# A static order for four interleaved layers on one core: overlapping durations in its planner, 28 more exponential pairs on VectorE, new due times

## The chip, the cores and the metric

The kernel runs on one core of a Trainium2 chip. The metric is the device time of one execution in microseconds. The kernel before took 2329.83 us (median of 3 runs, 2328.9 to 2332.01).

## The reference

```python
x = A_x                                     # 1 x 2048 x 1024, bf16
x = x + A(layernorm(x)); x = x + B(layernorm(x))
x = x + A(layernorm(x)); x = x + B(layernorm(x))

# A: linear attention, 32 heads of 32
q, k, v = split(x @ wqkv)
phi(t) = concat(softmax(t @ w_phi), softmax(-t @ w_phi))
kv = sum_s phi(k) v ; z = sum_s phi(k)
A = (phi(q) kv) / (phi(q) z + 1e-6) @ wo

# B: softmax attention, 32 heads of 32
p = softmax(q k^T / sqrt(32)) ; B = (p v) @ wo
```

Each layer pair has weights of its own kind (A's and B's), and both pairs use the same ones.

## The kernel before

The residual stream lies in SBUF, turned (features on partitions), as `xT`. The program is not written in the order in which it runs. The code makes a list of small steps (`op`: engine, assumed duration, what it needs, the buffers it takes, a due time called `prio`). Then `Sched.run` lays them out once, while the program is built: it follows an assumed clock, gives each engine, when it is free, the ready step with the earliest due time for which SBUF and PSUM have room, and writes the steps out in that order. On the chip each engine works through its own fixed list, held only by semaphores. So an assumed duration never runs on the chip. It only changes the order.

The work around the change is layer B's attention, done twice (once in each pair of layers):

- The 32 heads are 8 groups `g` of four, the 2048 queries 4 chunks `qc` of 512. One (qc, g) is a **turn**; there are 32 in each attention. A turn has two halves (`pp`), each of 32 **units**. A unit is a score block of 128 keys by 512 queries of one head.
- Three units make a score group: three matmuls of 32 rows each (L1124) into three PSUM banks. There are two such sets of three banks, used in turn. ScalarE takes the exponential of all three in one instruction of 1536 columns (L1140). There are 1366 of these, 683 in each attention, so a turn has 21 1/3 of them.
- Some units are handed to VectorE. The table `COUNT` says how many **pairs** of units each turn hands over, `HOST` after how many units of the half they are placed. A handed unit rides in a score group with two others, and ScalarE's instruction is then 1024 columns wide. VectorE reads its bank (the **take**, L1055). After two takes it finishes the pair by a polynomial on 1024 columns: L1063, L1067 twice, L1070, each needing the one before. The tiles between (`xg`, `xx`) exist once, the takes' result (`xu`) five times.
- The exponentials are multiplied into the values, and into ones for the denominator (L1172: four column groups of PE at once, in bank 6). After each half VectorE copies the sums out (L1188). The denominators go through small DMAs on SyncE's queue and a reciprocal (L1225), and L1232 divides.
- PE also does projections for coming turns through bank 7, again in four column groups (L499): K, Q and V (VectorE evacuates them in L940, L948, L964), the output projection, and in the first attention the next layer A's keys. Their due times are `KP`, `KGAP` (K), `VQ` (V), `QA`, `LATE` (Q), `OUT1`, `OP0`, `OGAP` (output), `AK` (next layer's keys), and, for the first projections of an attention, `LATER`; `OUT` is layer A's own output. The weights for them come by DMAs that POOL and SyncE issue (L601, L604).
- Where PE has nothing ready in an attention, the planner puts in a padding step (matmuls whose result is not used: `idle` and `idle_acc`, L1407 to L1416).

Before, the planner let an engine's next step begin when the one before it ended, with `dve_us(n) = n/960 + 0.15` and `act_us(n) = n/1200 + 0.064` us.

Of the kernel before, what the change touches and what calls it, by code (L numbers as in the profile page):

```python
# [11 lines left out]
ACT = mybir.ActivationFunctionType  # L12
# [34 lines left out]
LAT = {"PE": 0.2, "ACT": 0.08, "DVE": 0.1, "POOL": 0.2, "SP": 2.0, "AQ": 2.0, "GQ": 2.5}  # L47
SWITCH = 0.1
AGAIN = 0.2
RING = 0.5  # L50
TIE = 7
LOOK = 8
# [2 lines left out]
class Sched:  # L55
# [99 lines left out]
    def run(self):  # L155
# [6 lines left out]
        busy = {e: 0.0 for e in engines}  # L162
        mode = {e: None for e in engines}
        events = []
        n = 0
# [21 lines left out]
        t, left, order = 0.0, len(self.ops), []  # L187
        while left:
            moved = False
            for e in engines:  # L190
                if busy[e] > t + 1e-9 or not ready[e]:
                    continue
                skipped = []
                pick = None
                full = e == "PE" and self.live.get("E", 0) >= FULL
                while ready[e] and len(skipped) < 400:
                    item = heapq.heappop(ready[e])
                    if full and not item[3].first:
                        full = False
                        held = [i for i in ready[e] if i[3].drain] if not item[3].drain else []  # L200
                        best = min(held, key=lambda i: i[:3], default=None)
                        if best is not None and self._alloc(best[3].bufs):
                            ready[e].remove(best)
                            heapq.heapify(ready[e])
                            heapq.heappush(ready[e], item)
                            pick = best[3]
                            break
                    if item[3].along and (mode[e] != item[3].mode or item[3].rows[0] in rows) and item[3].prio > now - DUE:
                        skipped.append(item)
                        continue  # L210
                    if item[3].prio <= todo[front] + WINDOW and self._alloc(item[3].bufs):
                        pick = item[3]
                        break
                    skipped.append(item)
                for s in skipped:
                    heapq.heappush(ready[e], s)
                if pick is None and e == "PE" and self.idle is not None and self.live.get("S", 0):

                    recent = [r for r in recent if r[1] > t - SPELL]
                    worked = sum(r[1] - max(r[0], t - SPELL) for r in recent)  # L220
                    if worked >= KEEP * SPELL:
                        pass
                    elif self.bank_used[7]:

                        if accum:
                            pick = Op("PE", MM, LAT["PE"], self.idle_acc, (), 0.0, "c", 0)
                            left += 1
                    elif not self.live.get("fil", 0):
                        pick = Op("PE", MM, LAT["PE"], self.idle, (Buf("ps", 0, "idle", [(7,)]),), 0.0, "c", 0)
                        pick.bufs[0].left = 1  # L230
                        self.queue["idle"] = [list(pick.bufs), 0]
                        assert self._alloc(pick.bufs)
                        left += 1
                if pick is None:
                    continue
                if pick.first:
                    now = pick.prio
                if e == "PE":
                    recent.append((t, t + pick.dur))
                    if pick.accum is not None:  # L240
                        accum = pick.accum
                d = pick.dur
                if pick.along and (mode[e] != pick.mode or pick.rows[0] in rows):
                    d += AGAIN
                if e == "PE":
                    rows = pick.rows
                if pick.mode is not None:
                    if mode[e] is not None and mode[e] != pick.mode:
                        d += SWITCH
                    mode[e] = pick.mode  # L250
                pick.start = t
                if pick.fn not in (self.idle, self.idle_acc):
                    started[pick.prio] = started.get(pick.prio, 0) + 1
                while front < len(todo) - 1 and started.get(todo[front], 0):
                    started[todo[front]] -= 1
                    front += 1
                busy[e] = t + d
                order.append(pick)
                left -= 1
                moved = True  # L260
                n += 1
                heapq.heappush(events, (t + d, n, pick, True))
                n += 1
                lat = pick.lat
                if e in ("SP", "AQ", "GQ"):
                    ring = max(ring, t + d) + (lat - LAT[e]) * RING
                    lat = LAT[e] + ring - t - d + pick.slack
                heapq.heappush(events, (t + d + lat, n, pick, False))
            if moved:
                continue  # L270
            if not events:
                stuck = [(o.prio, o.eng, [(b.cls, b.at) for b in o.bufs]) for e in engines for _, _, _, o in ready[e]][:8]
                raise AssertionError(f"nothing can start at {t:.1f}: {left} left, {stuck}, live {self.live}")
            t = events[0][0]
            while events and events[0][0] <= t + 1e-9:
                _, _, o, own = heapq.heappop(events)
                if not own:
                    for b in o.bufs:
                        b.left -= 1
                        if b.left == 0:  # L280
                            self._release(b)
                for x in o.out:

                    if own != (x.eng == o.eng and x.eng not in ("SP", "AQ", "GQ")):
                        continue
                    x.ndep -= 1
                    if x.ndep == 0:
                        heapq.heappush(ready[x.eng], (not (x.first or x.along), x.prio - x.ahead, x.seq, x))
# [7 lines left out]
LONG = {"kT", "v", "slab", "slabk", "xn", "xn1", "kvacc", "kvm", "zm", "wnat"}  # L296
MODEST = {"slabk", "xn1", "e1", "vp1", "pkf", "lnw1", "w2o"}
NUMS = 2
LATER = ((20, 20, 0, 0), (20, 20, 0, 0))
VQ = (((1, 4.5), (36, 4), (70, 6)), ((1, 8), (70, 9), (140, 6)))  # L300
FULL = 5
OUT = (26, 22)
EARLY = (0.0, 0.0)
DUE = 0.0
BOOST = 20.0
EVAC = 20.0
QA = (90.0, 6.0)
KVG = 0.14
QUOTA = {"pk": 3, "pv": 2, "kv": 1, "ln": 2, "mm": 4, "cmp": 2, "bc": 4, "num": NUMS, "wt": 4, "fil": 2,
         "e": 6, "vp": 6, "e1": 4, "vp1": 4, "E": 6, "q2": 3, "kt": 3, "w2": 6, "w2o": 3, "oT": 27, "T": 4, "den": 2,  # L310
# [8 lines left out]
POW2_Z = 4  # L319
POW2_S = 0.07634790955  # L320
POW2_C = (-9.003200807141349, 20.025741504269316)
HOST = ((), (14,), (7, 18), (3, 12, 21), (2, 9, 16, 23))
SIDE = (2, 4)
HALF = 4
KGAP = (4, 6)
LATE = 10.0
KP = (0, 16, 56, 92, 122, 146, 170, 192)
BO = 225
OP0 = (243, 263, 287)
OGAP = (2.4, 2.4, 2.4)  # L330
COUNT = ((0,) * 3 + (2,) * 9 + (3,) * 5 + (2,) * 4 + (1,) * 4 + (2,) * 6 + (0,),
         (0,) + (2,) + (4, 3) * 12 + (2,) * 5 + (0,))
PAIRS = ((), ((0, 2),), ((0, 2), (1, 2)), ((0, 1), (0, 5), (1, 3)), ((0, 1), (0, 5), (1, 1), (1, 5)))
AK = ((0, 190), (1, 220), (2, 265))
OUT1 = ((163, 1.5), (176, 1.5), (251, 1.5))


def act_us(n):
# [3 lines left out]
def dve_us(n):  # L342
    return n / 960 + 0.15
# [6 lines left out]
def kernel(  # L350
# [148 lines left out]
            nc.tensor.matmul(out_[ks, :], lhsT=lhsT[:, ks], rhs=rhs, start=start, stop=stop,  # L499
                             tile_position=(0, 32 * k), skip_group_check=True)  # L500

    MM4 = 0.225

    def kind(pb):

# [182 lines left out]
    def a_keys(c, base, wk_s, wv_s, kv, banks, alone=False, step=0.1):  # L688
        xb, xv, fin = xnA[c]
        kv_b, kv_v, kv_last = kv  # L690
        for fc in range(2):
# [3 lines left out]
            for t in range(TB):  # L695
# [7 lines left out]
                if alone:  # L703
# [8 lines left out]
                red = op("DVE", dve_us(1024), lambda ev=ev, sv=sv: nc.vector.reduce_sum(  # L712
                    out=sv(), in_=ev().rearrange("p s (h d) -> p (s h) d", d=DH), axis=AX.X),
                    ex, [eb, sb_], pr)
                rc = op("DVE", 0.39, lambda sv=sv: nc.vector.reciprocal(out=sv(), in_=sv()), [red], [sb_], pr)
                pr_v = pr + (1.01 * step if alone else 0.01)
                vp, vpv = ps("fil" if alone else "pv", banks)
                v1 = mmg2(vp, vpv, lambda po, ts=ts: xv()[:, po, ts], lambda po, vw=vw: vw()[:, po, :],
# [77 lines left out]
    def split_hl(w_b, w_v, dep, prio):  # L796

        h_b, h_v = sb("hl", C512)
        s_b, s_v = sb("hl", C512)
        a = op("DVE", 0.42, lambda: nc.vector.tensor_copy(out=h_v(), in_=w_v()), [dep], [w_b, h_b], prio)  # L800
        b = op("DVE", dve_us(512), lambda: nc.vector.scalar_tensor_tensor(
            out=s_v(), in0=h_v(), scalar=hl[:, 0:1], in1=w_v(), op0=ALU.mult, op1=ALU.add),
            [a], [w_b, h_b, s_b], prio)
        return s_b, s_v, b
# [273 lines left out]
    def attention(base, kT, vT, q_of, gate, extra):  # L1078
# [69 lines left out]
        if True:  # L1148
            for qc, g in turns:
                T = []  # L1150
                end = (qc, g) == turns[-1]
                for pp in range(2):
# [5 lines left out]
                    for n, (d, u) in enumerate(order):  # L1158
                        prio = base + 10 * pos[(qc, g)] + 5 * pp + 0.5 * (n // 2)
                        if True:  # L1160
# [17 lines left out]
                            ebs = [e_of[us[0]][0]]  # L1178
                            if e_of[us[1]][0] is not ebs[0]:
                                ebs.append(e_of[us[1]][0])  # L1180
                            last = op("PE", 0.225, fn, flat([last, ex_of[us[0]], ex_of[us[1]], v_done[(kc % 4, g % 4 // 2)]]),
                                      [a_b, v_b, *ebs], prio - 1, mode="c")
                            last.accum = n != 15
                            last.drain = True
# [37 lines left out]
                    [T[k][2]], [c_b, T[k][0]], kb=2) for k in range(2) for i in range(2)]  # L1222
                for o in m:
                    o.slack = 1.5
                rc = op("DVE", 0.27, lambda c_v=c_v: nc.vector.reciprocal(out=c_v(), in_=c_v()), m, [c_b], prio)  # L1225
                aw = dma(prio, lambda c_v=c_v, at_d=at_d: nc.sync.dma_start(
                    out=at_d.rearrange("h (s c) -> (h s) c", c=16), in_=c_v()), [rc], [c_b], kb=8)
                bk = dma(prio, lambda r_v=r_v, at_d=at_d: nc.sync.dma_start(
# [221 lines left out]
```

## Time and profile before

| | before |
|---|---|
| median of 3 runs | 2329.83 us |
| the profiled execution, whole | 2329.07 us |
| its span, first to last instruction | 2327.3 us |
| granted TensorE clock | 0.997 |
| PE busy | 2223.1 us, 96% |
| ScalarE (ACT) busy | 2032.8 us, 87% |
| VectorE (DVE) busy | 1738.1 us, 75% |
| exponentials on ACT (L1140) | 1366, of them 308 with 1024 columns |
| takes on DVE (L1055) | 306, that is 153 pairs |

The busy share of an engine is the time in which at least one of its instructions is under way. ACT and DVE begin an instruction before the one in front has ended, so the durations of a group may add up to more than its busy time. PE's matmuls are pipelined, and their ends are modelled.

### The profile page before, as it was taken

What the parts mean: (1) busy time and instruction counts of PE and PEld (TensorE: products, weight loads), DVE (VectorE), ACT (ScalarE), POOL (GpSimd) and SP (SyncE); (2) the same over time, 40 slices, a digit from 0 to 9 for tenths busy, and PEclk for the clock granted to TensorE, in tenths of its full rate; (3) what the DMA queues carried; (4) which work ended last, traced back from release to release, by engine and by line L of the source; (5) the groups of instructions that cost most, each with busy time, mean ns of one, the idle gap of its engine ahead of it and who ended that gap; (6) DMA issues with size and microseconds to landing.
All of it is one profiled execution on the core that took longest, in us unless ns stands there. A gap on an engine that the chain in (4) does not pass through costs nothing. (4 is left out here: it accounts for less than half of the span.)

```text
span 2327.3 us, 68705 instructions
## 1 busy us (share of the span) xinstructions
PE 2223.1 (96%) x30156; PEld 872.5 (37%) x30220; DVE 1738.1 (75%) x2213; ACT 2032.8 (87%) x1921; POOL 182.8 (8%) x280
## 2 busy tenths in 40 slices
PE   7999999999999999999999999999999999999998
PEld 4443344444333333333333434433333333333333
DVE  7986762566678768577875776599999999888664
ACT  4436569999999999999997555799999999999997
POOL 0110000000011010111123200000000000100000
PEclk9999999999999999999999999999999999999999
DMA  9220101111132121122224100111110110201111
GB/s 204 55 62 1 33 15 39 41 37 39 45 83 76 48 76 56 62 98 70 83 90 140 43 16 13 24 34 32 30 34 21 40 31 25 66 29 32 46 37 36
DMA packets 124262, 118.80 MB, mean 51 GB/s; under 512 B 60729, under 2 KB 102713, under 8 KB 123577
## 3 DMA queue, kind: packets, MB, share of 16 engines
q1 hardware_dynamic: 105848, 60.38, 9.9%
q0 software_dynamic: 16032, 51.92, 7.9%
q8 instruction: 236, 3.87, 0.7%
q10 hardware_dynamic: 2080, 2.10, 0.3%
q14 instruction: 66, 0.53, 0.1%
HBM read 78.71 MB, written 14.14 MB: 40 GB/s over the span
## 5 line engine op out<-in xcount | busy, mean ns | idle before, releaser
L1140 ACT ACTIVATE arena<-psum 128x1536 bf16<-128x1536 f32 (+1 forms) x1366 | 1712.5, 1488 | 16.0 <-PE psum L1124 10.5
L1172 PE MATMUL psum<-arena 128*32 128x512 bf16 x4096 | 624.3, 384 | 4.8 <-DVE arena L1188 3.1
L1172 PE MATMUL psum<-arena,ones_bf 128*32 128x512 bf16 x4096 | 624.7, 384 | 1.8 <-issue 1.8
L499 PE MATMUL psum<-arena 128*32 128x512 bf16 (+1 forms) x10304 | 609.0, 349 | 4.0 <-DVE arena L1010 1.7
L1124 PE MATMUL psum<-arena 32*128 32x512 bf16 x4096 | 536.9, 382 | 57.5 <-ACT arena L1140 48.8
L495 PE MATMUL psum<-arena 128*128 128x512 bf16 (+1 forms) x1976 | 436.3, 368 | 15.2 <-issue 4.6
L1124 PEld LDWEIGHTS <-arena 32*128 32x128 bf16 x4096 | 179.0, 91 | 576.8 <-issue 567.9
L1067 DVE SCALAR_TENSOR_TENSOR arena<-arena 128x1024 f32<-128x1024 int32 (+1 forms) x306 | 373.6, 1221 | 11.5 <-PE psum L1124 1.5
L499 PEld LDWEIGHTS <-arena 128*32 128x32 bf16 x10304 | 234.9, 96 | 230.2 <-issue 115.9
L1055 DVE TENSOR_SCALAR arena<-psum 128x512 int32<-128x512 f32 x306 | 208.7, 686 | 104.7 <-PE psum L1124 96.1
L495 PEld LDWEIGHTS <-arena 128*128 128x128 bf16 x2032 | 189.5, 98 | 239.6 <-issue 50.3
L1172 PEld LDWEIGHTS <-arena 128*32 128x32 bf16 x4096 | 162.7, 95 | 229.9 <-issue 180.9
L1070 DVE SCALAR_TENSOR_TENSOR arena<-arena 128x1024 int32<-128x1024 f32 x153 | 186.3, 1218 | 2.8
L940 DVE CAST arena<-psum 128x512 bf16<-128x512 f32 x128 | 87.8, 686 | 121.0 <-PE psum L499 100.1
L1172 PEld LDWEIGHTS <-ones_bf 128*32 128x32 bf16 x4096 | 159.3, 95 | 26.5 <-issue 12.7
L601 POOL DMA_DIRECT2D arena<-in_B_wqkv_dram x46 | 40.8, 889 | 1289.3 <-ACT arena L1140 202.7
L1188 DVE COPY arena<-psum 128x512 f32<-128x512 f32 x126 | 86.5, 687 | 59.8 <-PE psum L1172 47.2
L708 ACT ACTIVATE arena<-psum 128x512 bf16<-128x512 f32 x80 | 43.1, 599 | 82.7 <-PE psum L495 61.0
L1063 DVE TENSOR_SCALAR arena<-arena 128x1024 int32<-128x1024 int32 x153 | 105.4, 689 | 5.0 <-PE psum L1172 1.5
L834 ACT ACTIVATE arena<-psum 128x512 bf16<-128x512 f32 x128 | 69.7, 596 | 33.0 <-PE psum L495 30.4
L499 PE MATMUL psum<-xT,onesD 128*32 128x512 bf16 x1044 | 97.1, 382 | 0.8 <-DVE arena L721 0.7
L587 DVE TENSOR_TENSOR arena<-xT,arena 128x1024 f32<-128x1024 bf16 x64 | 77.9, 1218 | 25.0 <-ACT arena L576 24.5
(108 smaller groups left out, 1400.6 us busy)
## 6 DMA issues: line engine op xcount, KB each, us to landing
arena<-rd SPq DMA_DIRECT2D x62, 256.0 KB
arena<-in_B_wqkv_dram POOLq DMA_DIRECT2D x58, 256.0 KB, 4.0
arena<-in_B_wo_dram POOLq DMA_DIRECT2D x40, 256.0 KB, 4.2
arena<-arena SPq DMA_DIRECT2D x256, 32.0 KB
arena<-wd_k POOLq DMA_DIRECT2D x32, 256.0 KB, 4.6
arena<-in_A_wqkv_dram POOLq DMA_DIRECT2D x32, 256.0 KB, 3.9
arena<-arena SPq DMA_DIRECT2D x96, 64.0 KB
out_dram<-arena SPq DMA_DIRECT2D x32, 128.0 KB
```

Source lines behind the costliest of these rows:

```text
L495: nc.tensor.matmul(out_, lhsT=lhsT, rhs=rhs, start=start, stop=stop, skip_group_check=True)
L499: nc.tensor.matmul(out_[ks, :], lhsT=lhsT[:, ks], rhs=rhs, start=start, stop=stop, tile_position=(0, 32 * k), skip_group_check=True)
L587: s1 = op("DVE", dve_us(1024), lambda pr=pr, w_v=w_v: nc.vector.tensor_tensor(out=w_v(), in0=xT[:, pr, csl(c)], in1=m_v().unsqueeze(1).to_ ...
L940: return op("DVE", dve_us(512), lambda: nc.vector.tensor_copy(out=dst(), in_=src()), [dep], bufs, prio)
L1055: o = op("DVE", dve_us(512), lambda: nc.vector.tensor_scalar(out=y_v()[:, k, :].bitcast(I32), in0=s_v()[:, x * C512:(x + 1) * C512], scala ...
L1063: last = op("DVE", 1024 / 1920 + 0.15, lambda: nc.vector.tensor_scalar(out=z_v().bitcast(I32), in0=y_v().bitcast(I32), scalar1=0x7FFFFF, s ...
L1067: last = op("DVE", dve_us(1024), lambda i=i, c=c: nc.vector.scalar_tensor_tensor(out=x_v(), in0=(x_v() if i else z_v().bitcast(I32)), scal ...
L1070: return op("DVE", dve_us(1024), lambda: nc.vector.scalar_tensor_tensor(out=y_v().bitcast(I32), in0=x_v(), scalar=POW2_S / BITS ** 2, in1= ...
L1124: nc.tensor.matmul(out=s_v()[:, x * C512:(x + 1) * C512], lhsT=kT[g][1]()[r, pp, d * P:(d + 1) * P], rhs=q_of[(qc, g)][1]()[r, (pp + j // ...
L1140: ex = op("ACT", act_us(w * C512), lambda s_v=s_v, e_v=e_v, w=w: nc.scalar.activation(out=e_v(), in_=s_v()[:, 0:w * C512], func=ACT.Exp, s ...
L1172: nc.tensor.matmul(out=a_v()[col:col + 32, :], lhsT=v_v()[:, kc % 4, o:o + DH] if what == 0 else ones_bf[:], rhs=ev()[:, x * C512:(x + 1) ...
L1188: cp = op("DVE", dve_us(512), lambda t_v=t_v, a_v=a_v: nc.vector.tensor_copy(out=t_v(), in_=a_v()), [last], [a_b, t_b], prio - 4)
```

## The change

The planner now frees DVE 0.085 us and ACT 0.012 us before a step's assumed end, and holds a dependent step of the same engine back by 0.03 and 0.13 us after it. Some assumed durations are set anew. `COUNT` hands over 28 more pairs: 15 in the first attention (57 to 72), 13 in the second (96 to 109). All due times listed above are set anew. No instruction is changed in itself; the work is the same but for the 28 pairs, and 381 padding steps of PE instead of 387. The lines of the kernel's body move down by 7 (L1140 becomes L1147).

```diff
+OVER = {"DVE": 0.085, "ACT": 0.012}
+NEXT = {"DVE": 0.03, "ACT": 0.13}
...
-                busy[e] = t + d
+                busy[e] = t + d - OVER.get(e, 0.0)
...
-                heapq.heappush(events, (t + d, n, pick, True))
+                if e in OVER:
+                    heapq.heappush(events, (busy[e], n, None, True))
+                    n += 1
+                heapq.heappush(events, (t + d + NEXT.get(e, 0.0), n, pick, True))
...
-VQ = (((1, 4.5), (36, 4), (70, 6)), ((1, 8), (70, 9), (140, 6)))
+VQ = (((9.3, 4.9), (45.9, 3.5), (68.0, 5.6)), ((6.9, 7.8), (67.1, 10.4), (149.7, 6.3)))
...
-OUT = (26, 22)
+OUT = (30.0, 20.7)
...
-HOST = ((), (14,), (7, 18), (3, 12, 21), (2, 9, 16, 23))
+HOST = ((), (14,), (5, 18), (3, 12, 19), (2, 11, 18, 23))
...
-COUNT = ((0,) * 3 + (2,) * 9 + (3,) * 5 + (2,) * 4 + (1,) * 4 + (2,) * 6 + (0,),
-         (0,) + (2,) + (4, 3) * 12 + (2,) * 5 + (0,))
+COUNT = ((0, 0, 0, 2, 3, 3, 4, 4, 4, 4, 3, 3, 4, 4, 4, 4, 3, 1, 2, 2, 2, 1, 1, 2, 0, 1, 2, 2, 2, 2, 2, 1),
+    (1, 2, 4, 4, 4, 4, 4, 4, 4, 4, 4, 3, 4, 3, 4, 4, 4, 4, 4, 3, 4, 4, 4, 4, 3, 3, 3, 3, 3, 3, 3, 0))
...
-    MM4 = 0.225
+    MM4 = 0.217
```

What it makes of the order is shown at two places. The first is ACT in the first attention, turns 8 and 9, from about the 166th exponential on. Before:

```order
L1140 ACTIVATE arena<-psum 128x1024 x2
L1140 ACTIVATE arena<-psum 128x1536 x8
L1140 ACTIVATE arena<-psum 128x1024 x2
L1140 ACTIVATE arena<-psum 128x1536 x9
L1140 ACTIVATE arena<-psum 128x1024 x2
L1140 ACTIVATE arena<-psum 128x1536 x9
```

ACT in the changed kernel, the same place:

```order
L1147 ACTIVATE arena<-psum 128x1536 x3
L1147 ACTIVATE arena<-psum 128x1024 x2
L1147 ACTIVATE arena<-psum 128x1536 x4
L1147 ACTIVATE arena<-psum 128x1024 x2
L1147 ACTIVATE arena<-psum 128x1536 x3
L1147 ACTIVATE arena<-psum 128x1024 x2
L1147 ACTIVATE arena<-psum 128x1536 x4
```

Two narrow exponentials used to come after eight or nine wide ones; now they come after three or four.

The second place is DVE in the second attention, between the 42nd and the 43rd of the copies that take the sums out (L1188). Before:

```order
L1188 COPY arena<-psum 128x512
L1055 TENSOR_SCALAR arena<-psum 128x512 x2
L1063 TENSOR_SCALAR arena<-arena 128x1024
L1067 SCALAR_TENSOR_TENSOR arena<-arena 128x1024 x2
L1225 RECIPROCAL arena<-arena 128x16
L1070 SCALAR_TENSOR_TENSOR arena<-arena 128x1024
L1188 COPY arena<-psum 128x512
```

DVE in the changed kernel, between the same two copies:

```order
L1195 COPY arena<-psum 128x512
L1062 TENSOR_SCALAR arena<-psum 128x512
L1070 TENSOR_SCALAR arena<-arena 128x1024
L1074 SCALAR_TENSOR_TENSOR arena<-arena 128x1024 x2
L1062 TENSOR_SCALAR arena<-psum 128x512
L1077 SCALAR_TENSOR_TENSOR arena<-arena 128x1024
L1062 TENSOR_SCALAR arena<-psum 128x512
L1232 RECIPROCAL arena<-arena 128x16
L1070 TENSOR_SCALAR arena<-arena 128x1024
L1074 SCALAR_TENSOR_TENSOR arena<-arena 128x1024 x2
L1077 SCALAR_TENSOR_TENSOR arena<-arena 128x1024
L1195 COPY arena<-psum 128x512
```

One pair's chain stood there, behind both of its takes; now there are two chains and three takes, and a take stands ahead of the last step of the first chain.

More of the change, by code (lines that the diff above doesn't have):

```diff
@@ L276, in run @@
                 _, _, o, own = heapq.heappop(events)
+                if o is None:
+                    continue
                 if not own:
@@ L298 @@
 NUMS = 2
-LATER = ((20, 20, 0, 0), (20, 20, 0, 0))
-VQ = (((1, 4.5), (36, 4), (70, 6)), ((1, 8), (70, 9), (140, 6)))
+LATER = ((21.3, 17.2, 0, 0), (25.4, 20, -4.9, -5.4))
+VQ = (((9.3, 4.9), (45.9, 3.5), (68.0, 5.6)), ((6.9, 7.8), (67.1, 10.4), (149.7, 6.3)))
 FULL = 5
-OUT = (26, 22)
+OUT = (30.0, 20.7)
 EARLY = (0.0, 0.0)
@@ L306 @@
 EVAC = 20.0
-QA = (90.0, 6.0)
+QA = (101.1, 5.8)
 KVG = 0.14
@@ L321 @@
 POW2_C = (-9.003200807141349, 20.025741504269316)
-HOST = ((), (14,), (7, 18), (3, 12, 21), (2, 9, 16, 23))
+HOST = ((), (14,), (5, 18), (3, 12, 19), (2, 11, 18, 23))
 SIDE = (2, 4)
 HALF = 4
-KGAP = (4, 6)
-LATE = 10.0
-KP = (0, 16, 56, 92, 122, 146, 170, 192)
+KGAP = (4.4, 6.5)
+LATE = 20.8
+KP = (0, 25.0, 52.2, 100.0, 122, 146, 173.7, 187.4)
 BO = 225
-OP0 = (243, 263, 287)
-OGAP = (2.4, 2.4, 2.4)
-COUNT = ((0,) * 3 + (2,) * 9 + (3,) * 5 + (2,) * 4 + (1,) * 4 + (2,) * 6 + (0,),
-         (0,) + (2,) + (4, 3) * 12 + (2,) * 5 + (0,))
+OP0 = (241.5, 264.7, 287.4)
+OGAP = (3.0, 2.8, 1.7)
+COUNT = ((0, 0, 0, 2, 3, 3, 4, 4, 4, 4, 3, 3, 4, 4, 4, 4, 3, 1, 2, 2, 2, 1, 1, 2, 0, 1, 2, 2, 2, 2, 2, 1),
+    (1, 2, 4, 4, 4, 4, 4, 4, 4, 4, 4, 3, 4, 3, 4, 4, 4, 4, 4, 3, 4, 4, 4, 4, 3, 3, 3, 3, 3, 3, 3, 0))
 PAIRS = ((), ((0, 2),), ((0, 2), (1, 2)), ((0, 1), (0, 5), (1, 3)), ((0, 1), (0, 5), (1, 1), (1, 5)))
-AK = ((0, 190), (1, 220), (2, 265))
-OUT1 = ((163, 1.5), (176, 1.5), (251, 1.5))
+AK = ((0, 190.1), (1, 231.9), (2, 263.0))
+OUT1 = ((163, 1.5), (182.0, 1.4), (247.9, 0.5))
 def act_us(n):
@@ L714, in a_keys @@
                     ex, [eb, sb_], pr)
-                rc = op("DVE", 0.39, lambda sv=sv: nc.vector.reciprocal(out=sv(), in_=sv()), [red], [sb_], pr)
+                rc = op("DVE", 0.35, lambda sv=sv: nc.vector.reciprocal(out=sv(), in_=sv()), [red], [sb_], pr)
                 pr_v = pr + (1.01 * step if alone else 0.01)
@@ L800, in split_hl @@
         a = op("DVE", 0.42, lambda: nc.vector.tensor_copy(out=h_v(), in_=w_v()), [dep], [w_b, h_b], prio)
-        b = op("DVE", dve_us(512), lambda: nc.vector.scalar_tensor_tensor(
+        b = op("DVE", 0.75, lambda: nc.vector.scalar_tensor_tensor(
             out=s_v(), in0=h_v(), scalar=hl[:, 0:1], in1=w_v(), op0=ALU.mult, op1=ALU.add),
@@ L1180, in attention @@
                                 ebs.append(e_of[us[1]][0])
-                            last = op("PE", 0.225, fn, flat([last, ex_of[us[0]], ex_of[us[1]], v_done[(kc % 4, g % 4 // 2)]]),
+                            last = op("PE", 0.217, fn, flat([last, ex_of[us[0]], ex_of[us[1]], v_done[(kc % 4, g % 4 // 2)]]),
                                       [a_b, v_b, *ebs], prio - 1, mode="c")
@@ L1224, in attention @@
                     o.slack = 1.5
-                rc = op("DVE", 0.27, lambda c_v=c_v: nc.vector.reciprocal(out=c_v(), in_=c_v()), m, [c_b], prio)
+                rc = op("DVE", 0.245, lambda c_v=c_v: nc.vector.reciprocal(out=c_v(), in_=c_v()), m, [c_b], prio)
                 aw = dma(prio, lambda c_v=c_v, at_d=at_d: nc.sync.dma_start(
```

## The prediction

> **What bounds the kernel now.** I read the page's totals first.
>
> ```profile
> span 2327.3 us, 68705 instructions
> ...
> PE 2223.1 (96%) x30156; PEld 872.5 (37%) x30220; DVE 1738.1 (75%) x2213; ACT 2032.8 (87%) x1921; POOL 182.8 (8%) x280
> ```
>
> Taken alone they name PE. So I cut the span where the stages change: a turn is 64 units, 21 1/3 exponentials, and the cuts are the starts of exponentials 0, 256, 363, 683, 726 and 1195 and the two ends of the layer-A work between the attentions. The view is busy time by stretch.
>
> ```profile
> core 0: us, PE busy (x) PEld busy (x) DVE busy (x) ACT busy (x) POOL busy (x), PEclk, DMA share, GB/s
> 0.00:342.70 342.70, 322.27 (x2912) 151.24 (x2951) 265.38 (x367) 173.66 (x287) 26.16 (x60) 1.00 0.27 63
> 342.70:678.90 336.20, 329.97 (x5346) 134.86 (x5346) 192.11 (x249) 329.24 (x263) 17.95 (x21) 0.99 0.18 45
> 678.90:811.40 132.50, 127.74 (x1733) 43.41 (x1733) 103.42 (x127) 131.86 (x108) 11.91 (x15) 1.00 0.21 60
> 811.40:1254.90 443.50, 417.50 (x6494) 149.74 (x6491) 317.26 (x391) 438.27 (x374) 86.18 (x127) 1.00 0.29 86
> 1254.90:1471.10 216.20, 210.39 (x1569) 89.55 (x1591) 156.53 (x216) 119.78 (x206) 17.19 (x31) 1.00 0.09 28
> 1471.10:1530.00 58.90, 55.26 (x865) 24.04 (x870) 34.86 (x42) 56.40 (x50) 2.65 (x3) 1.00 0.14 34
> 1530.00:2097.20 567.20, 544.09 (x7971) 200.01 (x7967) 522.27 (x640) 565.63 (x471) 17.23 (x21) 1.00 0.13 34
> 2097.20:2327.30 230.10, 215.88 (x3284) 79.64 (x3277) 146.23 (x187) 217.92 (x174) 3.52 (x4) 0.99 0.13 38
> ```
>
> From 342.7 to 1254.9 and from 1471.1 to the end ACT is busy 98 to 99.7% of nearly every stretch: the exponentials set the pace of both attentions. PE leads in the head (322 of 343) and between the attentions (210 of 216). DVE has a third to spare in the first attention, but in turns 2 to 23 of the second (1530 to 2097) it is already busy 522 of 567 us. That row decides this prediction.
>
> How much PE really has left: matmuls on four column groups start every 0.22 us, yet each is drawn 0.38 us long.
>
> ```profile
> 1601.55 0.39 PE L1172 MATMUL psum<-arena 128*32 128x512 bf16 x1
> ...
> 1601.77 0.38 PE L1172 MATMUL psum<-arena 128*32 128x512 bf16 x1
> ...
> 1601.99 0.38 PE L1172 MATMUL psum<-arena 128*32 128x512 bf16 x1
> ...
> 1602.38 0.39 PE L1124 MATMUL psum<-arena 32*128 32x512 bf16 x3
> 1602.70 0.39 PE L1172 MATMUL psum<-arena 128*32 128x512 bf16 x1
> ```
>
> The Trainium skill (Perfetto Trace Analysis, Identifying the Most-Contended Engine) calls matmul busy time a poor measure of headroom and takes weight-load busy time instead. By matmul busy time PE's 329.97 of 336.20 would leave the first twelve turns only 6 us; by the weight loads' 134.86 it would have far more. Starts 0.22 us apart under bars of 0.38 us agree with its warning, but a score group with its switch still takes 0.32 us.
>
> **The price of an exponential.** The groups by shape, then a row of the timeline in which all are 1536 wide:
>
> ```profile
> L1140 ACT ACTIVATE arena<-psum 128x1536 bf16<-128x1536 f32 x1058 | 1462.2, 1582 | 14.2 <-PE psum L1124 9.5 <-PE psum L1172 3.5 <-DVE arena L1067 0.4
> L1140 ACT ACTIVATE arena<-psum 128x1024 bf16<-128x1024 f32 x308 | 321.8, 1163 | 1.8 <-PE psum L1124 1.0 <-PE psum L1172 0.9
> ```
>
> ```profile
> 377.35 43.09 ACT L1140 ACTIVATE arena<-psum 128x1536 bf16<-128x1536 f32 x32 [1.98 <-PE psum L1124]
> ```
>
> 43.09/32 = 1.35 us from start to start, though one lasts 1.58: neighbours overlap. A 1024-wide one is 1582 - 1163 = 419 ns shorter. 28 pairs make 56 exponentials 1024 instead of 1536 wide, so ACT loses 56 x 0.42 = **23.5 us**. That is the ceiling of the gain by this route. The count of exponentials stays 1366.
>
> **The price of a pair on DVE.** Its instructions in a busy moment:
>
> ```profile
> 1601.55 0.68 DVE L940 CAST arena<-psum 128x512 bf16<-128x512 f32 x1
> 1602.15 0.68 DVE L1063 TENSOR_SCALAR arena<-arena 128x1024 int32<-128x1024 int32 x1
> 1602.88 0.69 DVE L1055 TENSOR_SCALAR arena<-psum 128x512 int32<-128x512 f32 x1
> 1603.48 1.22 DVE L1067 SCALAR_TENSOR_TENSOR arena<-arena 128x1024 f32<-128x1024 int32 x1
> 1604.62 0.68 DVE L1055 TENSOR_SCALAR arena<-psum 128x512 int32<-128x512 f32 x1
> 1605.64 1.38 DVE L1232 TENSOR_TENSOR arena<-arena 64x512 bf16<-64x512 f32 x2 [0.34 <-ACT arena L1140]
> 1607.05 1.23 DVE L1067 SCALAR_TENSOR_TENSOR arena<-arena 128x1024 f32<-128x1024 f32 x1
> 1608.32 1.22 DVE L1070 SCALAR_TENSOR_TENSOR arena<-arena 128x1024 int32<-128x1024 f32 x1
> 1609.46 0.69 DVE L1063 TENSOR_SCALAR arena<-arena 128x1024 int32<-128x1024 int32 x1
> ```
>
> Between independent instructions the step is 0.60 us for a 0.68 one (1601.55 to 1602.15) and 1.14 for a 1.22 one (1603.48 to 1604.62, 1608.32 to 1609.46). Where the next needs the result (L1067, then L1070 at 1608.32) it is 1.27. A pair is two takes, one L1063, two L1067 and one L1070: 3 x 0.61 + 3 x 1.14 = **5.25 us**, up to 0.13 more for each step that nothing separates. 28 pairs are 147 us of new DVE work, against 23.5 taken from ACT. So it must fit into DVE's free time, stretch by stretch.
>
> The Trainium skill (VectorE: DVE Perf Modes, The DRAIN you can't avoid) says that the next Vector instruction starts only when the pipe is empty, so that the step would be the whole duration: by that a pair is 5.7 us. The same page (Two Vector instructions with no wait between them) lets one start earlier unless its operands begin in another quadrant. The trace agrees with the second: 0.08 us of overlap in the rows above, and none in the L1232 pair, whose halves write different partitions (1.38 us for two).
>
> **Stage by stage**, pairs counted from the table of counts by turn:
>
> - First attention, turns 0 to 11: 18 pairs become 30. ACT would lose 24 x 0.42 = 10 us. But turns 6 to 9 take four pairs each instead of two:
>
> ```profile
> 514.80:622.60 107.80, 107.09 (x1723) 42.42 (x1716) 71.17 (x92) 107.80 (x87) 5.42 (x6) 1.00 0.18 45
> ```
>
>   Between those exponentials the new order has 7 1/2 pairs of chain work more (39 us) and five short instructions fewer (-3): DVE needs 71 + 36 = 107 of the present 107.8, while ACT falls to 101. DVE takes ACT's place and about 1 us is gained. Turns 3 to 5 have room and give 2 to 3. One stall stands out near the end of this stretch:
>
> ```profile
> 677.51 4.13 ACT L1140 ACTIVATE arena<-psum 128x1536 bf16<-128x1536 f32 x3 [2.63 <-PE psum L1124]
> ```
>
>   ACT waits 2.6 us for a score matmul there. It belongs to the old order, and I let it go. Together **-6**.
> - Turns 12 to 16: 15 pairs become 19. ACT 131.9 - 3.4 = 128.5; DVE 103.4 + 21 = 124.4, so it fits: **-2.5**. Turns 17 to 31: one pair fewer, **+1**.
> - Second attention, turns 0 and 1: one pair more, **-1**. Turns 24 to 31: 17 become 21. DVE 146 + 21 = 167 of 230, so ACT's loss of 3.4 counts: **-3.5**.
> - Second attention, turns 2 to 23: 77 pairs become 85. ACT falls to 565.6 - 16 x 0.42 = 559. DVE rises to 522.3 + 8 x 5.25 = 564. The two now stand within 1% of each other and of the present 567.2. What DVE still loses is bounded by what it waits for today:
>
> ```profile
> DVE arena L1055 <- PE psum L1124: 21.8, 39, 1.7
> PE psum L1124 <- ACT arena L1140: 20.1, 65, 0.6
> ```
>
>   None of it gives 564, all 21.8 us of it gives 586. A DVE that is behind finds its inputs ready, so I stay near the lower end and take 5 us: 569, **+2**. The eight pairs bring nothing here.
> - Head and the stretch between the attentions: the same instructions, laid out anew by the overlaps and by the new due times. PE idles 20 and 6 us there; that bounds a gain, and I allow as much loss. I take **0**. The projections, and the DMAs and POOL copies that feed them, move within turns in which PE does padding: in the order the padding steps are 387 before, 381 after. So moving a projection costs nothing until it lands where that padding is gone, turns 1 to 5 of the first attention, where a step would cost its 0.22 us in the open.
>
> Sum: -6 - 2.5 + 1 - 1 - 3.5 + 2 = -10. The profiled execution took 2329.07 us (span 2327.3 and 1.8 around it), 0.8 under the median of 2329.83. 2329.07 - 10 = **2319 us**.
>
> **Rivals.**
>
> *ACT's whole saving arrives.* The denser chains interleave so well that DVE hides them even in turns 2 to 23. For it: the order of the changed kernel puts takes between the chain's steps more often. Against it: 564 of 567. It gives 2329 - 23.5 = 2306, or a little less with the old stalls gone.
>
> *DVE late, slower than before.* A take that comes late holds its bank of the score half; PE cannot write the next scores there, and ACT stands still though its own half-work is done. Place: turns 2 to 23 and 6 to 9. If DVE keeps its present 21.8 us of waiting for scores, the stretch takes 586 instead of 569 (+17), and the first attention's 6 us go too: 2319 + 23 = 2342. It decides once DVE's waiting in turns 2 to 23 passes about 15 us (my 5 and the 10 gained).
>
> *A wash.* DVE loses some 12 us there, or the new due times cost the 8 us elsewhere that they might gain: 2325 to 2333.
>
> *No overlap on DVE.* If a step were the whole duration, a pair would cost 3 x 0.69 + 3 x 1.22 = 5.7 and the 522 could not be compressed: 568 + 22 = 590 in turns 2 to 23, 10 more in 6 to 9, about 2355. The rows at 1603.48 and 1604.62 speak against it. This is what the drain rule of the Trainium skill, above, would make of the change.
>
> *The pairs are not made.* Excluded: the new order has 362 takes against 306.
>
> **Chances.** Forecast (2310 to 2325) 0.50; whole saving 0.16; wash 0.16; late DVE 0.16; no overlap 0.02. A measurement here tells about 0.2% (4.7 us) from no change. Faster is the first two, 0.66; same 0.16; slower 0.18. The range goes from 2304, the full saving with 2 us of stalls, to 2336, halfway into the late DVE; that leaves out about 2 in 10.
>
> **What would show it.** In the profile after: exponentials 1004 x 1536 and 362 x 1024. In turns 2 to 23 of the second attention DVE above 97% busy, and ACT no longer at 99.7%, its idle time put down to score matmuls that waited for takes. The stretch as long as before within 5 us; turns 24 to 31 about 3.5 shorter; the first attention 7 shorter. Wrong would be ACT still at 99.7% in turns 2 to 23 (then 2306), DVE's wait for scores still 20 us and that stretch beyond 580 (then slower), or a change of over 6 us in the head or between the attentions, where I allow nothing.

## The result, and the profile after

The changed kernel takes 2308.31 us (median of 4 runs, 2307.73 to 2309.68), against 2329.93 before: a ratio of 0.9907 with a 95% interval of 0.989 to 0.9924, 21.6 us faster. The profiled execution has a span of 2307.9 us, 19.4 less than before.

The page's totals after:

```profile
span 2307.9 us, 68938 instructions
...
PE 2222.2 (96%) x30196; PEld 855.1 (37%) x30196; DVE 1859.0 (81%) x2381; ACT 2013.9 (87%) x1921; POOL 187.4 (8%) x280
```

PE is as busy as before, DVE 121 us more, ACT 19 us less: as much as the span. The same stretches as in the prediction, cut at the same exponentials:

```profile
core 0: us, PE busy (x) PEld busy (x) DVE busy (x) ACT busy (x) POOL busy (x), PEclk, DMA share, GB/s
0.00:340.30 340.30, 325.19 (x2958) 150.81 (x2962) 260.00 (x366) 173.07 (x286) 27.89 (x60) 0.99 0.28 63
340.30:665.60 325.30, 319.50 (x5205) 127.04 (x5201) 247.45 (x315) 320.42 (x263) 13.29 (x16) 0.99 0.16 40
665.60:796.50 130.90, 126.30 (x1721) 41.20 (x1717) 123.26 (x155) 129.87 (x109) 15.20 (x18) 1.00 0.25 70
796.50:1241.00 444.50, 422.18 (x6572) 149.59 (x6568) 310.14 (x387) 438.73 (x375) 90.43 (x129) 0.99 0.30 89
1241.00:1454.50 213.50, 210.59 (x1573) 88.55 (x1566) 154.70 (x216) 118.64 (x203) 16.85 (x30) 0.99 0.09 27
1454.50:1511.90 57.40, 55.27 (x849) 24.41 (x851) 39.09 (x47) 56.16 (x51) 1.76 (x2) 1.00 0.12 30
1511.90:2080.90 569.00, 549.90 (x8086) 197.84 (x8075) 557.27 (x688) 561.70 (x470) 18.40 (x22) 1.00 0.13 34
2080.90:2307.90 227.00, 213.31 (x3273) 75.68 (x3265) 167.03 (x212) 215.31 (x174) 3.53 (x4) 0.99 0.13 38
```

| stretch | before | after | change | forecast |
|---|---|---|---|---|
| head | 342.7 | 340.3 | -2.4 | 0 |
| first attention, turns 0 to 11 | 336.2 | 325.3 | -10.9 | -6 |
| turns 12 to 16 | 132.5 | 130.9 | -1.6 | -2.5 |
| turns 17 to 31 | 443.5 | 444.5 | +1.0 | +1 |
| between the attentions | 216.2 | 213.5 | -2.7 | 0 |
| second attention, turns 0 and 1 | 58.9 | 57.4 | -1.5 | -1 |
| turns 2 to 23 | 567.2 | 569.0 | +1.8 | +2 |
| turns 24 to 31 and the end | 230.1 | 227.0 | -3.1 | -3.5 |

In turns 2 to 23 both engines stand near their limit: ACT was busy 565.6 of 567.2 and is busy 561.7 of 569.0; DVE went from 522.3 to 557.3. The waits of that stretch (engine and line waited for: us in total, times, longest), first ACT's before, then those after:

```profile
ACT arena L1140 <- PE psum L1124: 1.3, 4, 0.5
```

```profile
ACT arena L1147 <- PE psum L1131: 6.4, 16, 1.0
...
DVE arena L1062 <- PE psum L1131: 1.3, 2, 0.7
```

DVE's takes waited 21.8 us for scores and now wait 1.3. DVE is behind, so what it needs is there; now ACT waits for scores instead, 6.4 us against 1.3. In six of its 16 waits, the longest among them (3.3 us in all), the scores begin 0.21 to 0.23 us after a take ends. And in turns 6 to 9 of the first attention DVE is busy practically throughout:

```profile
509.10:612.40 103.30, 101.60 (x1715) 40.76 (x1710) 102.43 (x131) 101.75 (x86) 2.65 (x3) 1.00 0.16 38
```

How densely DVE works in turns 2 to 23 of the second attention shows in a piece of its timeline:

```profile
1559.65 1.22 DVE L1074 SCALAR_TENSOR_TENSOR arena<-arena 128x1024 f32<-128x1024 f32 x1
1560.79 0.68 DVE L1062 TENSOR_SCALAR arena<-psum 128x512 int32<-128x512 f32 x1
1561.39 1.21 DVE L1077 SCALAR_TENSOR_TENSOR arena<-arena 128x1024 int32<-128x1024 f32 x1
1562.52 0.68 DVE L1062 TENSOR_SCALAR arena<-psum 128x512 int32<-128x512 f32 x1
1563.12 1.40 DVE L1239 TENSOR_TENSOR arena<-arena 64x512 bf16<-64x512 f32 x2
1564.55 0.69 DVE L1070 TENSOR_SCALAR arena<-arena 128x1024 int32<-128x1024 int32 x1
```

A take (L1062) stands between two dependent steps of a chain (L1074 at 1559.65, L1077 at 1561.39), so each begins 0.08 us before the one ahead has ended.

### The profile page after: what moved, and what is told of

Same layout as the page of the kernel before. It is cut to its first block, busy times and chain, and to the rows that moved or that the text cites. A ratio compares the mean times of both kernels' runs of the same rounds, so it can differ in the third digit from the quotient of the medians.

```text
span 2307.9 us, 68938 instructions
## 1 busy us (share of the span) xinstructions
PE 2222.2 (96%) x30196; PEld 855.1 (37%) x30196; DVE 1859.0 (81%) x2381; ACT 2013.9 (87%) x1921; POOL 187.4 (8%) x280
## 4 chain that ended last, share of the span: by engine, by line
PE 21%; ACT 14%; DVE 11%; issue 5%; DMA 1%; SPq 0%; DVEq 0%; ACTq 0%; POOL 0%; POOLq 0%
ACT arena L1147 13%; PE psum L502 8%; PE psum L506 5%; PE psum L1179 4%; PE psum L1131 4%; DVE arena L1074 3%; DVE arena L1062 2%; DVE arena L1077 1%; DVE arena L1070 1%; DVE arena L1239 1%; DVE arena L1195 1%; DMA arena<-arena 1%; DVE arena L947 0%; PE psum L884 0%; DMA arena<-rd 0%
## 5 line engine op out<-in xcount | busy, mean ns | idle before, releaser
L1147 ACT ACTIVATE arena<-psum 128x1536 bf16<-128x1536 f32 (+1 forms) x1366 | 1697.1, 1420 | 19.4 <-PE psum L1131 16.1
L1074 DVE SCALAR_TENSOR_TENSOR arena<-arena 128x1024 f32<-128x1024 int32 x362 | 441.3, 1219 | 10.9 <-DVE arena L1070 0.6
L502 PE MATMUL psum<-arena 128*128 128x512 bf16 (+1 forms) x2032 | 443.8, 369 | 5.7 <-DVE arena L1216 3.4
L1131 PEld LDWEIGHTS <-arena 32*128 32x128 bf16 x4096 | 160.1, 91 | 559.7 <-issue 549.9
L1062 DVE TENSOR_SCALAR arena<-psum 128x512 int32<-128x512 f32 x362 | 244.6, 683 | 60.3 <-PE psum L1131 52.3
L1077 DVE SCALAR_TENSOR_TENSOR arena<-arena 128x1024 int32<-128x1024 f32 x181 | 220.2, 1216 | 2.6
L1070 DVE TENSOR_SCALAR arena<-arena 128x1024 int32<-128x1024 int32 x181 | 124.0, 685 | 4.3 <-DMA arena<-arena 1.6
L719 DVE TENSOR_REDUCE arena<-arena 128x32 f32<-128x1024 bf16 x64 | 77.2, 1214 | 33.1 <-ACT arena L715 32.3
L1195 DVE COPY arena<-psum 128x512 f32<-128x512 f32 x126 | 86.1, 683 | 20.5 <-PE psum L1179 20.0
```

Source lines behind the costliest of these rows:

```text
L502: nc.tensor.matmul(out_, lhsT=lhsT, rhs=rhs, start=start, stop=stop, skip_group_check=True)
L1062: o = op("DVE", dve_us(512), lambda: nc.vector.tensor_scalar(out=y_v()[:, k, :].bitcast(I32), in0=s_v()[:, x * C512:(x + 1) * C512], scala ...
L1070: last = op("DVE", 1024 / 1920 + 0.15, lambda: nc.vector.tensor_scalar(out=z_v().bitcast(I32), in0=y_v().bitcast(I32), scalar1=0x7FFFFF, s ...
L1074: last = op("DVE", dve_us(1024), lambda i=i, c=c: nc.vector.scalar_tensor_tensor(out=x_v(), in0=(x_v() if i else z_v().bitcast(I32)), scal ...
L1077: return op("DVE", dve_us(1024), lambda: nc.vector.scalar_tensor_tensor(out=y_v().bitcast(I32), in0=x_v(), scalar=POW2_S / BITS ** 2, in1= ...
L1131: nc.tensor.matmul(out=s_v()[:, x * C512:(x + 1) * C512], lhsT=kT[g][1]()[r, pp, d * P:(d + 1) * P], rhs=q_of[(qc, g)][1]()[r, (pp + j // ...
```

## The experiments

After the result the theory was the prediction's: a pair pays where DVE has room, and nothing in turns 2 to 23. The rival: the gain is that of the new order, and the pairs matter little. "Change" below is against the kernel before, timed beside each run (its medians were 2328.1 to 2329.9).

**The three parts of the change, one at a time.** x1: only the pairs.

```diff
 # before.py, with the new HOST and COUNT; planner and due times of before
+HOST = ((), (14,), (5, 18), (3, 12, 19), (2, 11, 18, 23))
+COUNT = ((0, 0, 0, 2, 3, 3, 4, 4, 4, 4, ...
```

> The kernel before with only the tables of pairs (COUNT, HOST) of the changed kernel; planner and due times as before. If room on DVE decides (my theory), the pairs by themselves bring most of the gain in the first attention (24 exponentials narrower in turns 0 to 11, about -8) and in turns 24 to 31 of the second (-3), and in turns 2 to 23, laid out with DVE's instructions assumed too long, the dense chains cost more than the changed kernel's +2: about +6. Together 2325, between 2318 and 2331. If the new order brings the gain (the rival), the pairs alone bring nothing or lose: 2330 or more. If ACT's whole saving arrives wherever a pair is made: 2306.

Measured 2344.36 us, 16.2 **slower** (ratio 1.007, 1.0053 to 1.0086). x2: only the planner.

```diff
 # after.py, with HOST, COUNT and every due time of before
+OVER = {"DVE": 0.085, "ACT": 0.012}
+NEXT = {"DVE": 0.03, "ACT": 0.13}
+    MM4 = 0.217   # and the other new durations
```

> The kernel before with only the planner's overlaps and the new assumed durations; pairs and due times as before. My theory: ACT is at its limit in both attentions and the order gives little: 2326, between 2320 and 2332. The rival (the order brings the gain): 2315 or less.

Measured 2330.36, 2.2 slower (1.0013, 1.0004 to 1.0023). x3: only the due times.

```diff
 # before.py, with the new LATER, VQ, OUT, QA, KGAP, LATE, KP, OP0, OGAP, AK, OUT1
```

> The kernel before with only the new due times; pairs and planner as before. My theory: 2329, between 2324 and 2335, since ACT's load is the same. If the due times bring the part of the gain that I did not forecast (the head and the stretch between the attentions, about 5 us, and some of turns 0 to 11): 2320 to 2324.

Measured 2323.10, 5.0 faster (0.9979, 0.997 to 0.9989). x4: all but the pairs.

```diff
 # after.py
-HOST = ((), (14,), (5, 18), (3, 12, 19), (2, 11, 18, 23))
+HOST = ((), (14,), (7, 18), (3, 12, 21), (2, 9, 16, 23))
-COUNT = ((0, 0, 0, 2, 3, 3, ...
+COUNT = ((0,) * 3 + (2,) * 9 + ...
```

> The changed kernel with the tables of pairs (COUNT, HOST) of before. My theory: the ACT time that the pairs took off where DVE had room comes back, about 10 us in turns 0 to 16 of the first attention, 1 in turns 0 and 1 and 3.4 in turns 24 to 31 of the second, less 1 in turns 17 to 31; turns 2 to 23 stay as they are. 2308 + 13 = 2321, between 2316 and 2326. The rival (the order brings the gain): 2312 or less.

Measured 2330.26, 2.1 slower (1.0009, 1.0 to 1.0018). Of the four only x2 lies in its range; x3 lies in that of the alternative it named, though its 5 us are not in the stretch between the attentions (217.2 against 216.2) but in turns 0 to 11 (331.8 against 336.2) and the head. Both theories fell: neither the pairs alone nor all of the new order without them gains. x9 completes the square: the changed kernel with the planner of before.

```diff
 # after.py
-OVER = {"DVE": 0.085, "ACT": 0.012}
-NEXT = {"DVE": 0.03, "ACT": 0.13}
+OVER = {"DVE": 0.0, "ACT": 0.0}
+NEXT = {"DVE": 0.0, "ACT": 0.0}
+    MM4 = 0.225   # and the other durations of before
```

> The changed kernel (its pairs and due times) laid out by the planner of before: no overlap, no hold of dependent steps, the old assumed durations. After the first runs my theory is that the pairs pay only in an order that knows how fast DVE is: turns 2 to 23 of the second attention 10 to 15 us longer than the changed kernel's 569, turns 24 to 31 and 12 to 16 about 4 each: 2308 + 20 = 2328, between 2322 and 2342. The rival (the due times make the pairs pay, the planner is not needed): 2308 to 2314.

Measured 2356.19, 27.6 slower (1.0122, 1.0104 to 1.0141), beyond its range, although turns 2 to 23 came out as expected (583.8). With the new due times:

| change in us | pairs of before | 28 more pairs |
|---|---|---|
| planner of before | -5.0 (x3) | +27.6 (x9) |
| planner with overlaps | +2.1 (x4) | -21.6 (the changed kernel) |

So with the new due times 28 pairs cost 33 us under the planner of before and give 24 under the new one. That the 24 lie close to the prediction's 23.5 is chance: from x4 to the changed kernel turns 2 to 23 give 3.3 us for eight pairs, and turns 17 to 31 give 7.9 with one pair fewer. ACT's busy time falls by 18.9 us in all, 0.67 a pair instead of 0.84.

One corner is missing: the new planner with the 28 pairs and the due times of before was not run. And x4 and x9 take the changed kernel's due times as they are; whether other due times would let the planner of before bear the pairs is not tested.

Where the pairs cost, x1 shows. Nearly all that it loses against before, 15 of 16 us, lies in turns 2 to 23. It has 85 pairs there as the changed kernel has, DVE and ACT are busy as long, but the stretch is 13 us longer; this is its row, and then its two largest ACT waits:

```profile
1528.50:2110.80 582.30, 551.51 (x8131) 205.75 (x8123) 556.19 (x681) 560.97 (x471) 17.27 (x21) 1.00 0.12 32
```

```profile
ACT arena L1140 <- PE psum L1172: 17.9, 14, 3.0
ACT arena L1140 <- PE psum L1124: 1.5, 3, 0.8
```

ACT does not wait for scores (1.5 us) but for the accumulating matmuls (17.9), 14 times. The longest of these on the timelines of DVE, PE and ACT, x1:

```profile
1919.82 1.23 DVE L1070 SCALAR_TENSOR_TENSOR arena<-arena 128x1024 int32<-128x1024 f32 x1
1921.30 0.69 DVE L1055 TENSOR_SCALAR arena<-psum 128x512 int32<-128x512 f32 x1 [0.25 <-PE psum L1124]
1921.91 0.68 DVE L1063 TENSOR_SCALAR arena<-arena 128x1024 int32<-128x1024 int32 x1
1922.51 0.68 DVE L1188 COPY arena<-psum 128x512 f32<-128x512 f32 x1
```

```profile
1921.12 1.05 PE L499 MATMUL psum<-arena 128*32 128x512 bf16 x16
1921.99 0.39 PE L1172 MATMUL psum<-arena 128*32 128x512 bf16 x2
1922.00 0.39 PE L1172 MATMUL psum<-arena,ones_bf 128*32 128x512 bf16 x2
1923.24 0.38 PE L1172 MATMUL psum<-arena 128*32 128x512 bf16 x1 [0.86 <-DVE arena L1188]
```

```profile
1923.75 1.45 ACT L1140 ACTIVATE arena<-psum 128x1536 bf16<-128x1536 f32 x1 [3.01 <-PE psum L1172]
```

Read from DVE on: the last step of a pair ends at 1921.05. The kernel puts a half's handed pairs last among its accumulations, so only now can PE close the half with that pair's four matmuls. PE does so at 1921.99, without an idle moment before: a projection (L499) stands ahead in its list. DVE copies the sums out at 1922.51, behind a take and an L1063 of its own list. The copy frees bank 6, PE begins the next half's accumulations (1923.24), the first of the six exponential buffers comes free, and ACT goes on after 3.0 us.

So here the place in the lists, and not a wait for DVE, sets when the half closes. Counted on the timelines over the 44 halves of turns 2 to 23, the four matmuls of one pair stand alone as the closing of 29 halves in x1, 29 in x9, 12 in the changed kernel and 10 before. In the median they begin 0.6 us after the end of the latest pair in x1 and x9, and 3.0 in the changed kernel. ACT's wait for accumulations is 20.5 us in x9 and does not appear among the waits of that stretch in the changed kernel. Why the planner of before places the closings so is argued, not shown: it took a pair for 5.70 us of DVE (by `dve_us`) where the prediction's rows give 5.25, and set PE's fixed list by that.

x9 also lost 18 us between the attentions (231.5 against 213.5). There the eight partial output projections (their additions on DVE are L1017) come after the last exponential; in the changed kernel they come before it.

**The hold of dependent steps.** x10 keeps the overlaps and takes the hold away.

```diff
 # after.py
-NEXT = {"DVE": 0.03, "ACT": 0.13}
+NEXT = {"DVE": 0.0, "ACT": 0.0}
```

> The changed kernel without the planner's hold of dependent steps (NEXT all zero), with its overlaps. My theory: knowing DVE's rate is what counts, and the hold is a detail of 0.1 us: 2308 to 2314. The rival (the chains must be known to be slow when nothing separates them, so that takes are put between): 2318 or more, with turns 2 to 23 over 575.

Measured 2321.53, 7.1 faster than before (0.997, 0.9958 to 0.9982), so 14 of the 21.6 us are gone: the rival's total, though not at the place it named. Turns 2 to 23 take 571.7; turns 12 to 16 lose most, 138.3 against 130.9. There ACT waits 5.1 us for scores and 2.8 for a step of a pair (L1074), against 0.5 and 0.2 in the changed kernel. The hold counts; I did not test why there, nor whether it is DVE's 0.03 us or ACT's 0.13.

**How many pairs turns 2 to 23 bear.** Three kernels change only the 22 numbers of these turns; x5 has 88 pairs, x6 66, x12 the 77 of before.

```diff
 # after.py, turns 2 to 23 of the second attention in COUNT
-4, 4, 4, 4, 4, 4, 4, 4, 4, 3, 4, 3, 4, 4, 4, 4, 4, 3, 4, 4, 4, 4   # 85
+4, 4, 4, 4, 4, 4, 4, 4, 4, 4, 4, 4, 4, 4, 4, 4, 4, 4, 4, 4, 4, 4   # x5: 88
+3, 3, 3, 3, 3, 3, 3, 3, 3, 3, 3, 3, 3, 3, 3, 3, 3, 3, 3, 3, 3, 3   # x6: 66
+4, 3, 4, 3, 4, 3, 4, 3, 4, 3, 4, 3, 4, 3, 4, 3, 4, 3, 4, 3, 4, 3   # x12: 77
```

> The changed kernel with four pairs in each of turns 2 to 23 of the second attention (88 instead of 85). My theory (DVE is the limit there, busy 557 of 569 us): three pairs more are 3 x 5.25 = 16 us of DVE work in a stretch with 12 us free, so the stretch grows by 4 to 16 us: 584 at most, whole kernel 2312 to 2324. The rival (ACT is still the limit, 562 of 569): 2.5 us shorter, 2306.

> The changed kernel with three pairs in each of turns 2 to 23 of the second attention (66 instead of 85). My theory: ACT is the limit there again, with 19 x 2 x 0.42 = 16 us more than with 85 pairs: 562 + 16 = 578, plus 1 to 3 of stalls, so the stretch is 579 to 581 and the kernel 2318 to 2321. A theory by which DVE alone sets the stretch also at 66 pairs would have it shorter, not longer.

> The changed kernel with the pairs of before (77 instead of 85) in turns 2 to 23 of the second attention alone. My theory: with 77 pairs ACT is the limit there (562 + 16 x 0.42 = 568), with 85 DVE, and both give the same time; the stretch is 567 to 571, the kernel 2306 to 2311. If the eight pairs paid as the others do: 2315. If they cost: 2303 or less.

Measured: x5 2310.72 (0.9917, 0.99 to 0.9933), x6 2312.71 (0.9926, 0.9911 to 0.9941), x12 2306.22 (0.9904, 0.9888 to 0.9921). The stretch's row in x6, x12 and x5 (the changed kernel's stands above):

```profile
1503.90:2079.50 575.60, 557.81 (x8231) 201.83 (x8224) 471.85 (x576) 574.50 (x470) 18.45 (x22) 1.00 0.13 34
```

```profile
1508.70:2078.20 569.50, 551.96 (x8135) 198.49 (x8130) 526.21 (x642) 567.22 (x470) 18.57 (x23) 1.00 0.13 34
```

```profile
1509.10:2083.20 574.10, 552.07 (x8127) 199.38 (x8119) 566.01 (x703) 559.60 (x471) 18.45 (x22) 1.00 0.13 34
```

With 66 pairs the stretch is ACT's (574.5 of 575.6), with 88 DVE's (566.0 of 574.1), and between them lies a flat bottom: 569.5 at 77, 569.0 at 85. The eight pairs there bring nothing, as forecast. x5's stretch grew by 5, in its range, though the kernel came out just under the range. x6's direction is right and its size too large: a pair takes 0.67 us off ACT's busy time here, not 0.84. Part of the difference is in the measure. From start to start the median step is 1.33 us between two wide exponentials and 0.90 between two narrow ones, before as after, which is the prediction's price; but the bars overlap, so an exponential that begins a little late leaves no gap in the busy time. x6's profiled execution was also its fastest (2306.83), so its stretch may be a little short.

**Does the gain belong to one lucky order?** x7 and x8 take another draw of the planner's random spread of durations (1% at most).

```diff
-TIE = 7
+TIE = 8    # x7: after.py; x8: before.py
```

> The changed kernel with another draw of the planner's random spread of assumed durations (TIE 8 for 7): the same work, pairs and due times in a slightly other order. It measures how far a stretch moves by the order alone. My theory: within 6 us, 2308 to 2314, no stretch more than 4 us off. If the gain belongs to this one order and not to its rules (the rival): 2318 or more.

> The kernel before with another draw of the planner's random spread (TIE 8 for 7). My theory: 2325 to 2336. If the order of before was itself a chosen draw, it loses more than 6 us.

Measured x7 2306.09 (0.9904, 0.9889 to 0.9919), x8 2327.01 (0.999, 0.9981 to 0.9999). Another draw of either kernel keeps its time, so the gain does not hang on this draw; x7 came 2 us under its range. x8 also settles the head: 339.1 us, and 337 to 341 in every other kernel of this study. The 342.7 was the peculiarity of the one draw and execution, not a cost that the change removed.

**More pairs where DVE has room.** x11 adds eight to turns 17 to 24 of the first attention and three to turns 24 to 31 of the second.

```diff
 # after.py, COUNT: turns 17 to 24 of the first, 24 to 31 of the second attention
-1, 2, 2, 2, 1, 1, 2, 0      3, 3, 3, 3, 3, 3, 3, 0
+2, 3, 3, 3, 2, 2, 3, 1      4, 3, 4, 3, 4, 3, 3, 0
```

> The changed kernel with 11 more pairs where the profile shows room on DVE: one more in each of turns 17 to 24 of the first attention (DVE busy 310 of 444 us there, ACT 439), and three more in turns 24 to 31 of the second. My theory: ACT is the limit in both places and DVE has room, so each pair gives 0.84 us: 2308 - 9 = 2299, between 2295 and 2304. The rival (PE, with its projections, has taken ACT's place there, or the untuned due times cost as much): 2306 or more.

Measured 2330.69, all of the gain lost (1.001, 1.0 to 1.002). Turns 17 to 31 did get shorter, 440.0 against 444.5; but x6 and x9, with the changed kernel's pairs there, take 440.2 and 439.8, so this is not shown to be the pairs. Turns 24 to 31 of the second attention stay as long (227.6 against 227.0). And the stretch between the attentions grew from 213.5 to 239.1. Its row in x11, and in it the additions of the eight partial output projections:

```profile
1236.00:1475.10 239.10, 224.17 (x1957) 96.33 (x1974) 164.57 (x230) 119.43 (x206) 37.24 (x61) 1.00 0.18 52
```

```profile
L1016 DVE TENSOR_TENSOR arena<-xT,psum 128x512 f32<-128x512 bf16 x8 | 5.5, 687 | 15.1 <-PE psum L505 15.1
```

All eight stand here, behind the last exponential, with their weights' DMAs (share 0.18 against 0.09); in the changed kernel none does. The projections share bank 7 and DVE with the last chunk's layer-A keys and come right behind them. The keys' last addition (L763, in x11 L762) begins at 1206.9 in the changed kernel, 34 us ahead of the last exponential (1241.0). In x11 it begins at 1246.2, 10 us after the last exponential (1236.0), and in x9 at 1250.5 (1250.0). In x11 the projections' additions then follow one by one, 2.3 us and more apart, from 1248.2 to 1266.5. Why the keys came so late is not shown. Free time on DVE was there; what moved behind it was not free.

## Why the prediction was right or wrong

- **What bounds each stretch: right.** ACT in both attentions, DVE taking its place in turns 2 to 23 and 6 to 9; x5, x6 and x12 show both limits and the flat bottom.
- **Turns 2 to 23, +2: right in sum (+1.8), by two errors that cancel, which is luck.** "DVE rises to 522.3 + 8 x 5.25 = 564" with 5 us of waiting; measured 557.3 busy and 11.7 not busy. Of the 11.7 some 4 us are waits, as forecast; most of the rest (6 us) are gaps under 0.06 us, mainly in front of steps that need the one before. The prediction named their price (up to 0.13 us a step) and left it out of its sum. A pair's price in busy time depends on how full DVE already is: 4.9 us from 66 to 77 pairs ((526.2 - 471.9)/11), 3.9 from 77 to 85. (x5's row holds 15 DVE instructions more than the changed kernel's, not the 18 of three pairs, so it gives no price.)
- **Turns 0 to 11, -6 against -10.9: the step that failed is "DVE needs 71 + 36 = 107".** I took the 71 us as rigid. They count each instruction at its whole duration wherever idle time follows it; set close, the old instructions overlap too. Over turns 6 to 9 the overlaps were 2.5 us of 72.8 us of durations before, and are 8.4 of 111.1 after. DVE was busy 102.4 of 103.3, so it did take ACT's place, and turns 6 to 9 gave 4.0, not 1 (103.3 against 107.3, cut at the same exponentials). About half of the gain of turns 0 to 11 is the new order, which I priced at nothing: x4, without the pairs, takes 331.2 there, and x3, with the due times alone, 331.8. (x4 loses elsewhere, most in turns 17 to 31, 452.4 against 443.5 before; why stays open.)
- **Head and the stretch between, 0: each moved by less than 3 us.** The first belongs to the draw or the execution of before (x8): no other kernel's head reaches 341, so these 2.4 us of the gain are luck. Between the attentions 212.6 to 214.8 us stand wherever the planner's overlaps and the new due times come together (save x11) and 215.6 to 217.2 in x1, x2, x3 and x8, where one or both are missing; so I put these 2 to 3 us to both together, from one profiled execution each.
- **"The new order costs or brings nothing": true of the planner alone (x2), wrong as an account of the change.** I priced the pairs by engine time and the order at nothing. With the new due times the same pairs make +27.6 under the planner of before and -21.6 under the new one, and with the planner and due times of before +16.2.
- **The slower rival's place was wrong.** I expected a late take to hold its score bank. In the two slowest, x1 and x9, the halves are closed late, right behind a pair, and ACT waits for the buffers behind that: 17.9 us in x1, against 1.5 for scores.
- **The count of exponentials was off by two.** 28 pairs add 56 narrow ones to 308: 364, and 1002 wide, as measured, not 362 and 1004. The prediction took the count of takes; two more are narrow without a pair. Nothing else hangs on it.
- **Size.** -10 forecast, -19.4 measured in the span: 4.9 of the miss in turns 0 to 11, 5.1 in the head and between the attentions.

## What to carry to other kernels

When an engine close to its limit gets work from another, add up both engines stretch by stretch, in steps from start to start and not in busy time; the gain ends where their sums meet. In a program laid out in advance, the durations that the layout assumes are part of such a change: with the same pairs and due times this kernel lost 28 us under the planner of before and won 22 under the one that knows how steps overlap. Before adding more, look at what stands last in the stretch: work pushed past its end is paid for in the next one, where another engine is the limit.

## What the hardware showed that I had not expected

Two DVE steps that depend on each other take 1.26 to 1.27 us from start to start where independent ones take 1.14. In the planner this difference is 0.085 us of overlap and 0.03 of hold; without the holds, DVE's and ACT's together, the kernel takes 2321.53 us instead of 2308.31 (x10). The independent step of 0.60 us for 512 columns and 1.14 for 1024 fits what the Trainium skill gives (Vector Engine (DVE) Microarchitecture Reference, Measured stream behaviour on trn2): 1.0417 ns a column and about 75 ns an instruction after overlap, 0.61 and 1.14 us by estimate. The Trainium skill's rule on DVE operands that begin in another quadrant (VectorE: DVE Perf Modes, Two Vector instructions with no wait between them) is borne out again at 1563.12: the two halves of L1239 take 1.40 us together, without overlap, in the densest stretch as well.
